# Retention followed by a token-choosing feed-forward: one hand-written order over all 24 chunks

## The chip, the cores and the metric

The kernel runs on one core of a Trainium2 chip. The metric is the device time of one execution in microseconds (us). The core has a matrix engine (TensorE, PE in the profile, with its weight loads PEld), a vector engine (VectorE, DVE), an engine for activations and copies (ScalarE, ACT), a general engine (GpSimd, POOL) and a queue engine for transfers (SyncE, SP). Each engine works through its own queue of instructions in order and waits at the head of it for the semaphores of others. Both SyncE and GpSimd issue DMAs here.

## The reference, cut to what matters

```python
def _attn_ref(q, k, v):                      # each (4, 8, 768, 64): batch, head, token, width
    gamma = 1.0 - 2.0 ** (-5.0 - np.arange(H))
    for t in range(S):
        state = gamma * state + k[:, :, t] (outer) v[:, :, t]
        y[:, :, t] = 1/sqrt(D) * q[:, :, t] @ state

def _moe_ref(x, w_gate, w1, w2, capacity):   # x: (4, 768, 512), the heads side by side
    scores = x @ w_gate                      # one score per token
    out = x.copy()
    for b in range(B):
        top_idx = the 128 tokens of the highest scores
        ye = np.maximum(x[b, top_idx] @ w1, 0.0) @ w2        # 512 -> 1024 -> 512
        g = 1 / (1 + exp(-scores[b, top_idx]))
        out[b, top_idx] = x[b, top_idx] + g[:, None] * ye
```

So each batch is a linear recurrence over 768 tokens with a decaying 64x64 state per head, and then a choice of 128 of the 768 tokens by a score, for which a small feed-forward is added. The whole batch's scores must be known before the choice.

## The kernel before, in words

The 768 tokens of a batch are cut into 6 chunks of 128 tokens. With 4 batches there are 24 chunks. The decay is put into scaled values: `gneg` scales v on its way in, `gpos` scales y on its way out.

*Loads.* k and q of a batch are loaded and cast to bf16 by GpSimd's queue, into tiles with 128 partitions of 6 consecutive tokens each; batch 0 in two halves of 4 heads, the others whole. v is loaded by SyncE's queue in f32, for batch 0 in six pieces by chunk (packets of 256 bytes), for the others whole. `wgb`, the score weights `w_gate` repeated on 128 partitions, comes by SyncE's queue between the third and the fourth piece of v, and w1 and w2 by GpSimd's queue.

*Transposes.* `transpose_qk` (lines 163-173) turns two heads of k or q of a batch into `KT` or `QT` with 12 TensorE transposes and one ScalarE copy; 8 such units make a batch ready.

*A chunk* (`attention`, lines 179-248):
- GpSimd scales v to `Vg` (L183).
- TensorE makes the scores k·q of 8 heads into PSUM tile `pa` (L191), in two halves of 4 matmuls; DVE masks each half to `Am` (L194).
- TensorE forms y in `py` from the earlier state (L201) and from `Am` and `Vg` (L204); DVE scales it to `xo` (L226), SyncE stores it, ScalarE keeps a bf16 copy `xs` (L231).
- TensorE transposes k's rows to `pk` (L210), ScalarE copies them to `Kn`, TensorE adds to the state `U` (L217) and ScalarE copies `U` to `ubd` (L223). The last chunk of a batch leaves this out.
- DVE multiplies `xo` by `wgb` and adds it up to the score column `s6` (the group named `junk`, L235). TensorE spreads the column as a row (`pr`, L238), ScalarE copies it to `srow` (L239), DVE compares all scores so far with this chunk's (`G`, L242), TensorE counts (`pc`, L247), and DVE subtracts the counts from `rank` (L248).

*The feed-forward* (`ffn`, `ffn_store`, lines 250-316) follows a batch's six chunks: DVE builds the choice matrices `P` from `rank`, TensorE gathers the chosen rows (`px`, L267), ScalarE copies them to `xeT`, TensorE gathers places and scores (`pa`, L274), goes up (`ph`, 32 matmuls, L291, with ReLU copies to `hT` on ScalarE) and down (`pe`, 8 matmuls of 512 columns, L304); DVE adds the gated result to `ot` (L310), and GpSimd scatters the rows with an indirect DMA (L312).

*What sets the order.* The program is written batch by batch and chunk by chunk, with the next batch's loads and transposes between the chunks. A list scheduler takes these instructions and sets each engine's order by itself, with the program's order as priority; it allots the slots of the tile pools. The names `psT`, `psA`, `psY`, `psU` and `psF` are pools in PSUM, with 2, 2, 1, 1 and 2 slots of a bank each.

Of the kernel before, what the change touches and what calls it, by code (L numbers as in the profile page):

```python
# [36 lines left out]
def kernel(  # L37
# [27 lines left out]
    ld = ctx.enter_context(tc.tile_pool(name="ld", bufs=B))  # L65
    work = ctx.enter_context(tc.tile_pool(name="work", bufs=3))
    bat = ctx.enter_context(tc.tile_pool(name="bat", bufs=2))
    psT = ctx.enter_context(tc.tile_pool(name="psT", bufs=2, space=bass.MemoryType.PSUM))
    psA = ctx.enter_context(tc.tile_pool(name="psA", bufs=2, space=bass.MemoryType.PSUM))
    psY = ctx.enter_context(tc.tile_pool(name="psY", bufs=1, space=bass.MemoryType.PSUM))  # L70
    psU = ctx.enter_context(tc.tile_pool(name="psU", bufs=1, space=bass.MemoryType.PSUM))
    psF = ctx.enter_context(tc.tile_pool(name="psF", bufs=2, space=bass.MemoryType.PSUM))
# [4 lines left out]
    def load_qk(src, name, tiles, b, h0, h1):  # L77
        if b not in tiles:
            tiles[b] = ld.tile([128, H, J * D], BF, tag=name, name=f"{name}{b}")
        nc.gpsimd.dma_start(tiles[b][:, h0:h1, :],  # L80
                            _view(src[b, h0], [[J * D, 128], [S * D, h1 - h0], [1, J * D]]))

    def load_v(b, c0, c1):
        if b not in vtiles:
            vtiles[b] = ld.tile([128, H, NC, D], FT, tag="v", name=f"v{b}")
        if c1 - c0 == NC:
            ins = nc.sync.dma_start(vtiles[b].rearrange("p h c d -> p (h c) d"),
                                    _view(v[b], [[D, 128], [C * D, H * NC], [1, D]]))
            tc.keep_in_program_order(ins)
        else:  # L90
            for c in range(c0, c1):
                nc.sync.dma_start(vtiles[b][:, :, c, :],
                                  _view(v[b, 0, c * C], [[D, 128], [S * D, H], [1, D]]))

    for h0 in (0, H // 2):
        load_qk(k, "k", ktiles, 0, h0, h0 + H // 2)
        load_qk(q, "q", qtiles, 0, h0, h0 + H // 2)
    load_v(0, 0, 3)

# [51 lines left out]
    load_v(0, 3, NC)  # L151

    w1 = consts.tile([128, ND, F], BF)
    w2 = consts.tile([128, NF, Dm], BF)

# [3 lines left out]


    QTs, KTs = {}, {}

    def transpose_qk(tiles, name, dst, b, dd):
        if b not in dst:
            dst[b] = bat.tile([128, ND, S], BF, tag=name, name=f"{name}{b}")
        tv = tiles[b].rearrange("p h (j d) -> p h j d", j=J)
        pt = psT.tile([128, J, 128], BF, tag="T")
        for j in range(J):
            for sub in range(2):
                nc.tensor.transpose(pt[sub * 64:sub * 64 + 64, j, :], tv[:, 2 * dd + sub, j, :], ident,  # L170
                                    tile_position=(0, sub * 64))
        nc.scalar.activation(dst[b][:, dd, :].rearrange("f (p j) -> f p j", j=J),  # L172
                             pt.rearrange("f j p -> f p j"), AF.Copy)

    for dd in range(ND):
        transpose_qk(ktiles, "KT", KTs, 0, dd)
        transpose_qk(qtiles, "QT", QTs, 0, dd)

    def attention(b, c, st):
        QT, KT = QTs[b], KTs[b]  # L180
        t = slice(c * C, (c + 1) * C)
        Vg = work.tile([128, H, D], BF, tag="Vg")
        nc.gpsimd.tensor_mul(Vg, vtiles[b][:, :, c, :], gneg[:, c, :, None].to_broadcast([128, H, D]))  # L183
        vf = Vg.rearrange("p h d -> p (h d)")

        Ams = []
        for sub in range(2):
            pa = psA.tile([128, ND, 128], FT, tag="A")
            r = slice(sub * 64, sub * 64 + 64)
            for dd in range(ND):  # L190
                nc.tensor.matmul(pa[:, dd, :], KT[r, dd, t], QT[r, dd, t],  # L191
                                 start=True, stop=True)
            Am = work.tile([128, ND, 128], BF, tag=f"Am{sub}")
            nc.vector.tensor_mul(Am, pa, causal4)  # L194
            Ams.append(Am)

        py = psY.tile([128, H, D], FT, tag="y")
        pyf = py.rearrange("p h d -> p (h d)")
        for dd in range(ND):
            if c:  # L200
                nc.tensor.matmul(pyf[:, dd * 128:(dd + 1) * 128], QT[:, dd, c * C:(c + 1) * C],  # L201
                                 Ubd[(c - 1) % 2][:, dd, :], start=True, stop=False)
            for sub in range(2):
                nc.tensor.matmul(py[:, 2 * dd + sub, :], Ams[sub][:, dd, :], Vg[:, 2 * dd + sub, :],  # L204
                                 start=(c == 0), stop=(c == 0 or sub == 1))

        if c < NC - 1:
            pk = psT.tile([128, J, 128], BF, tag="T")
            for dd in range(ND):
                nc.tensor.transpose(pk[:, dd, :], KT[:, dd, t], ident)  # L210
            Kn = work.tile([128, ND, 128], BF, tag="Kn")
            nc.scalar.activation(Kn, pk[:, 0:ND, :], AF.Copy)  # L212
            if c == 0:
                st["U"] = psU.tile([128, ND, 128], FT, tag="U", name="U")
            U = st["U"]
            for dd in range(ND):
                nc.tensor.matmul(U[:, dd, :], Kn[:, dd, :],  # L217
                                 vf[:, dd * 128:(dd + 1) * 128],
                                 start=(c == 0 and dd == 0), stop=(c == NC - 2 and dd == ND - 1),
                                 skip_group_check=True)  # L220
            for sub in range(2):
                r = slice(sub * 64, sub * 64 + 64)
                nc.scalar.activation(Ubd[c % 2][r, :, r], U[r, :, r], AF.Copy)  # L223

# [4 lines left out]
        for sc in scatters:  # L229
            tc.declare_no_dep(base.ins, sc.ins, reason="rows of different batches")  # L230
        nc.scalar.activation(st["xs"][:, c, :], xof, AF.Copy)  # L231

        s6, srow, rank = st["s6"], st["srow"], st["rank"]
        junk = work.tile([128, Dm], FT, tag="junk")
        nc.vector.scalar_tensor_tensor(out=junk, in0=xof, scalar=1.0, in1=wgb, op0=ALU.mult,  # L235
                                       op1=ALU.mult, accum_out=s6[:, c:c + 1])
        pr = psF.tile([128, 512], FT, tag="F")
        nc.tensor.transpose(pr[:, 0:128], s6[:, c:c + 1].to_broadcast([128, 128]), identf)  # L238
        nc.scalar.activation(srow[:, c * C:(c + 1) * C], pr[:, 0:128], AF.Copy)  # L239
        n = (c + 1) * C  # L240
        G = work.tile([128, S], BF, tag="G")
        nc.vector.scalar_tensor_tensor(out=G[:, 0:n], in0=srow[:, 0:n], scalar=s6[:, c:c + 1],  # L242
                                       in1=before[:, S - n:], op0=ALU.is_ge, op1=ALU.mult,
                                       accum_out=st["racc"][:, c:c + 1])
        pc = psF.tile([128, 512], FT, tag="F")
        for j in range(c + 1):
            nc.tensor.matmul(pc[:, j:j + 1], G[:, j * C:(j + 1) * C], ones, start=True, stop=True)  # L247
        nc.vector.tensor_sub(rank[:, 0:c + 1], rank[:, 0:c + 1], pc[:, 0:c + 1])  # L248

    def ffn(b, st):  # L250
        s6, rank, xs = st["s6"], st["rank"], st["xs"]
        nc.vector.tensor_add(rank, rank, st["racc"])
        P = bat.tile([128, NC, 128], BF, tag="P")
        for c in range(NC):
            nc.vector.tensor_scalar(P[:, c, :], sel, rank[:, c:c + 1], None, op0=ALU.is_equal)  # L255
        aux = bat.tile([128, NC, 5], BF, tag="aux")
        rem = bat.tile([128, NC], FT, tag="rem")
        nc.gpsimd.tensor_copy(aux[:, :, 0:2], place_i)
        nc.gpsimd.tensor_copy(aux[:, :, 2], s6)
        nc.gpsimd.tensor_sub(rem, s6, aux[:, :, 2])  # L260
        nc.gpsimd.tensor_copy(aux[:, :, 3], rem)
        nc.gpsimd.tensor_sub(aux[:, :, 4], rem, aux[:, :, 3])

        px = psF.tile([128, 512], FT, tag="F")
        for dd in range(ND):
            for c in range(NC):
                nc.tensor.matmul(px[:, dd * 128:(dd + 1) * 128], xs[:, c, dd * 128:(dd + 1) * 128],  # L267
                                 P[:, c, :], start=(c == 0), stop=(c == NC - 1))
        xeT = bat.tile([128, ND, 128], BF, tag="xeT")
        nc.scalar.activation(xeT, px.rearrange("p (a b) -> p a b", b=128), AF.Copy)  # L270

        pa = psF.tile([128, 512], FT, tag="F")
        for c in range(NC):
            nc.tensor.matmul(pa[:, 0:5], P[:, c, :], aux[:, c, :], start=(c == 0), stop=(c == NC - 1))  # L274
        auxs = bat.tile([128, 5], FT, tag="auxs")
        nc.vector.tensor_copy(auxs, pa[:, 0:5])
        idx = bat.tile([128, 1], I32, tag="idx")
        nc.vector.scalar_tensor_tensor(out=idx, in0=auxs[:, 0:1], scalar=float(b * S),
                                       in1=auxs[:, 1:2], op0=ALU.add, op1=ALU.add)
        ssel = bat.tile([128, 1], FT, tag="ssel")  # L280
        nc.vector.reduce_sum(ssel, auxs[:, 2:5], axis=mybir.AxisListType.X)
        gate = bat.tile([128, 1], FT, tag="gate")
        nc.scalar.activation(gate, ssel, AF.Sigmoid)

        hT = bat.tile([128, NF, 128], BF, tag="hT")
        for half in range(2):
            ph = psF.tile([128, 512], FT, tag="F")
            for f4 in range(4):
                ff = half * 4 + f4
                for dd in range(ND):  # L290
                    nc.tensor.matmul(ph[:, f4 * 128:(f4 + 1) * 128], w1[:, dd, ff * 128:(ff + 1) * 128],  # L291
                                     xeT[:, dd, :], start=(dd == 0), stop=(dd == ND - 1))
# [85 lines left out]
```

## Time and profile before

| what | value |
|---|---|
| time, median of 3 runs | 168.11 us (167.86 to 168.26) |
| the profiled execution | 169.33 us |
| its span, first to last instruction | 167.5 us |
| TensorE busy | 118.1 us (71%), 1412 matmuls |
| VectorE busy | 96.2 us (57%) |
| ScalarE busy | 81.5 us (49%) |
| GpSimd busy | 48.1 us (29%) |
| mean granted TensorE clock | 0.772 of full |
| read from HBM / written | 23.33 MB / 7.34 MB |

The profile comes from one execution. In its page, the second part cuts the span into 40 slices of 4.19 us; a digit is the busy share in tenths, and PEclk the granted TensorE clock in tenths. A group of instructions is written as line, engine, operation, output<-input, shapes and count, then busy time and the mean of one in ns. A timeline row gives the start, the time, the engine and the line, and in brackets the idle time before it with what ended it. TensorE's busy time counts the latency of matmuls that overlap, so it looks fuller than it is.

### The profile page before, as it was taken

How to read it: one execution, taken by the hardware profiler on the slowest of the kernel's cores; microseconds unless marked ns; L12 is line 12 of the kernel's file. 1: busy time of each engine (PE TensorE's matmuls, PEld its weight loads, DVE VectorE, ACT ScalarE, POOL GpSimd, SP SyncE). 2: the span in 40 equal slices, each digit the busy share in tenths (PEclk: the TensorE clock that was granted, in tenths of full speed). 3: DMA queues.
4: the chain of work that ended last, by engine and by line, in shares of the span. 5: the costliest groups of instructions: out<-in, count | busy, mean ns of one | idle time of the engine just before them, and what ended most of it. 6: DMA issues, size and time to landing. Idle time of an engine off the chain costs nothing.

```text
span 167.5 us, 3545 instructions
## 1 busy us (share of the span) xinstructions
PE 118.1 (71%) x1412; PEld 88.1 (53%) x1412; DVE 96.2 (57%) x254; ACT 81.5 (49%) x164; POOL 48.1 (29%) x76
## 2 busy tenths in 40 slices
PE   0028570999999559988867995998479977454870
PEld 0016450676666339766644974766349645234840
DVE  3400031655648896159879708599697299876010
ACT  3015461457554304599981146697821668520230
POOL 7972000626222400072251105222530063010002
PEclk9999996555555555999995579599956999955598
DMA  5999999999999999613111892111301013220001
GB/s 124 175 213 195 191 191 204 207 247 250 251 254 253 230 265 250 148 65 126 70 71 55 217 216 72 63 65 67 125 0 67 0 67 125 86 87 15 4 0 63
DMA packets 24751, 22.50 MB, mean 134 GB/s; under 512 B 6944, under 2 KB 20768, under 8 KB 24736
## 3 DMA queue, kind: packets, MB, share of 16 engines
q0 software_dynamic: 10240, 9.44, 32.9%
q1 hardware_dynamic: 14496, 12.85, 28.8%
q8 instruction: 11, 0.18, 0.4%
q14 instruction: 4, 0.03, 0.1%
HBM read 23.33 MB, written 7.34 MB: 183 GB/s over the span
## 4 chain that ended last, share of the span: by engine, by line
PE 38%; DVE 16%; DMA 14%; ACT 13%; issue 12%; POOL 3%; POOLq 1%; DVEq 0%; ACTq 0%
DMA q<-in_q_dram 13%; PE pt L170 6%; DVE G L242 6%; PE px L267 5%; PE pa L191 5%; PE ph L291 5%; ACT ubd L223 4%; DVE Am L194 4%; DVE junk L235 3%; PE pe L304 3%; PE U L217 3%; PE pr L238 3%; PE py L201 2%; PE py L204 2%; ACT srow L239 2%
## 5 line engine op out<-in xcount | busy, mean ns | idle before, releaser
L194 DVE TENSOR_TENSOR Am<-pa,causal 128x512 bf16<-128x512 f32 x48 | 32.2, 685 | 21.4 <-PE pa L191 19.8
L183 POOL TENSOR_TENSOR Vg<-v,gneg 128x512 bf16<-128x512 f32 x24 | 25.8, 1076 | 53.1 <-PE py L204 21.6
L191 PE MATMUL pa<-QT,KT 64*128 64x128 bf16 x192 | 23.7, 269 | 3.5 <-ACT QT L172 1.8
L242 DVE SCALAR_TENSOR_TENSOR G<-srow,s,before 128x128 bf16<-128x128 f32 (+5 forms) x24 | 20.3, 847 | 9.0 <-ACT srow L239 8.6
L170 PE MATMUL pt<-ident,k 128*64 128x128 bf16 x192 | 13.6, 263 | 11.8 <-DMA k<-in_k_dram 11.1
L226 DVE TENSOR_TENSOR xo<-py,gpos 128x512 f32<-128x512 f32 x24 | 16.5, 686 | 7.8 <-PE py L204 7.6
L231 ACT ACTIVATE xs<-xo 128x512 bf16<-128x512 f32 x24 | 15.1, 628 | 9.9 <-DVE xo L226 9.8
L223 ACT ACTIVATE ubd<-U 64x256 bf16<-64x256 f32 x40 | 15.1, 377 | 9.5 <-PE U L217 8.5
L170 PE MATMUL pt<-ident,q 128*64 128x128 bf16 x192 | 13.6, 270 | 8.3 <-DMA q<-in_q_dram 8.1
L204 PE MATMUL py<-Vg,Am 128*128 128x64 bf16 x192 | 18.3, 218 | 1.2 <-DVE Am L194 0.9
L172 ACT ACTIVATE QT<-pt 128x768 bf16<-128x768 bf16 x16 | 13.0, 813 | 9.8 <-PE pt L170 9.7
L235 DVE SCALAR_TENSOR_TENSOR junk<-xo,wgb 128x512 f32<-128x512 f32 x24 | 17.4, 724 | 0.0
L191 PEld LDWEIGHTS <-KT 64*128 64x128 bf16 x192 | 12.3, 111 | 9.3 <-issue 4.5
L204 PEld LDWEIGHTS <-Am 128*128 128x128 bf16 x192 | 14.9, 115 | 4.2 <-DVE Am L194 2.1
L170 PEld LDWEIGHTS <-k 128*64 128x64 bf16 x192 | 8.8, 131 | 14.8 <-DMA k<-in_k_dram 11.5
L172 ACT ACTIVATE KT<-pt 128x768 bf16<-128x768 bf16 x16 | 12.9, 809 | 6.2 <-PE pt L170 6.0
L201 PE MATMUL py<-ubd,QT 128*128 128x128 bf16 x80 | 14.6, 247 | 1.4 <-DVE xo L226 0.9
L170 PEld LDWEIGHTS <-q 128*64 128x64 bf16 x192 | 9.2, 137 | 10.6 <-DMA q<-in_q_dram 8.7
L312 POOL DMA_INDIRECT out_dram<-ot,idx x4 | 4.4, 1098 | 35.6 <-DVE ot L310 35.6
L212 ACT ACTIVATE Kn<-pk 128x512 bf16<-128x512 bf16 x20 | 11.9, 600 | 4.6 <-PE pk L210 4.5
L267 PE MATMUL px<-P,xs 128*128 128x128 bf16 x96 | 12.5, 303 | 1.3 <-DVE P L255 1.3
L310 DVE SCALAR_TENSOR_TENSOR ot<-pe,gate,xe 128x512 f32<-128x512 f32 x4 | 3.0, 751 | 16.6 <-PE pe L304 16.6
(67 smaller groups left out, 172.1 us busy)
## 6 DMA issues: line engine op xcount, KB each, us to landing
out_dram<-xo SPq DMA_DIRECT2D x24, 256.0 KB, 2.0
k<-in_k_dram POOLq DMA_DIRECT2D x3, 768.0 KB, 18.4
q<-in_q_dram POOLq DMA_DIRECT2D x3, 768.0 KB, 22.4
w<-in_moe_w_dram POOLq DMA_DIRECT2D x2, 1024.0 KB, 29.9
v<-in_v_dram SPq DMA_DIRECT2D x6, 256.0 KB, 13.9
k<-in_k_dram POOLq DMA_DIRECT2D x2, 384.0 KB, 10.5
q<-in_q_dram POOLq DMA_DIRECT2D x2, 384.0 KB, 12.4
wgb<-in_moe_w_gate_dram SPq DMA_DIRECT2D x1, 256.0 KB, 11.9
```

Of the source, the lines that this page charges most:

```text
L170: nc.tensor.transpose(pt[sub * 64:sub * 64 + 64, j, :], tv[:, 2 * dd + sub, j, :], ident, tile_position=(0, sub * 64))
L172: nc.scalar.activation(dst[b][:, dd, :].rearrange("f (p j) -> f p j", j=J), pt.rearrange("f j p -> f p j"), AF.Copy)
L183: nc.gpsimd.tensor_mul(Vg, vtiles[b][:, :, c, :], gneg[:, c, :, None].to_broadcast([128, H, D]))
L191: nc.tensor.matmul(pa[:, dd, :], KT[r, dd, t], QT[r, dd, t], start=True, stop=True)
L194: nc.vector.tensor_mul(Am, pa, causal4)
L201: nc.tensor.matmul(pyf[:, dd * 128:(dd + 1) * 128], QT[:, dd, c * C:(c + 1) * C], Ubd[(c - 1) % 2][:, dd, :], start=True, stop=False)
L204: nc.tensor.matmul(py[:, 2 * dd + sub, :], Ams[sub][:, dd, :], Vg[:, 2 * dd + sub, :], start=(c == 0), stop=(c == 0 or sub == 1))
L223: nc.scalar.activation(Ubd[c % 2][r, :, r], U[r, :, r], AF.Copy)
L226: nc.vector.tensor_mul(xo, py, gpos[:, c, :, None].to_broadcast([128, H, D]))
L235: nc.vector.scalar_tensor_tensor(out=junk, in0=xof, scalar=1.0, in1=wgb, op0=ALU.mult, op1=ALU.mult, accum_out=s6[:, c:c + 1])
L242: nc.vector.scalar_tensor_tensor(out=G[:, 0:n], in0=srow[:, 0:n], scalar=s6[:, c:c + 1], in1=before[:, S - n:], op0=ALU.is_ge, op1=ALU.mul ...
L267: nc.tensor.matmul(px[:, dd * 128:(dd + 1) * 128], xs[:, c, dd * 128:(dd + 1) * 128], P[:, c, :], start=(c == 0), stop=(c == NC - 1))
```

## The change

The list scheduler is switched off by `manual_schedule`: each engine now takes its instructions in the order in which the program writes them. The program is rewritten as one pipeline over n = 0 to 25 (24 chunks and two more rounds), in which each round works on several chunks. The functions of a chunk are cut apart: `scale_v` works two chunks ahead, `scores_kq` and `k_rows` one ahead, `values`, `state` and `score` on chunk n, `score_rows` and `compare` one behind and `count` two behind.

The two half masks become one DVE instruction of 128x1024 over a two-bank tile (`psA` has one slot). The row transpose and the counts share one tile in a new pool `psR` with one slot, and `psF` goes from 2 slots to 1. The feed-forward becomes nine pieces, of which up to three are put at the end of a round from round 14 on; the last batch's nine all follow in round 25.

Batch 0's k and q are loaded in two halves of 64 partitions, which is tokens 0-383 and 384-767, instead of two halves of heads. Its transposes then come in 16 units of half the width. v's pieces 3-5 are issued right behind pieces 0-2, and so ahead of `wgb`. Batches 1 and 2 are asked for at the start, batch 3 in round 5, w1 and w2 in round 3, and the `ld` pool goes from 4 buffers to 3.

```diff
+    ctx.enter_context(tc.manual_schedule())
...
-    for h0 in (0, H // 2):
-        load_qk(k, "k", ktiles, 0, h0, h0 + H // 2)
-        load_qk(q, "q", qtiles, 0, h0, h0 + H // 2)
     load_v(0, 0, 3)
+    for p0 in (0, 64):
+        load_qk(k, "k", ktiles, 0, p0, p0 + 64)
+        load_qk(q, "q", qtiles, 0, p0, p0 + 64)
+    load_v(0, 3, NC)
...
     wgb = consts.tile([128, Dm], FT)
     nc.sync.dma_start(wgb, _view(moe_w_gate, [[0, 128], [1, Dm]]))
...
-    load_v(0, 3, NC)
...
+    load_batch(1)
+    load_batch(2)
...
+        return [choose, gather_a, gather_b, places, rows, lambda: up(0), lambda: up(1), down, store]
...
+    units = {}
+    for b in range(1, B):
+        order = [("KT", dd) for dd in range(ND)] + [("QT", dd) for dd in range(ND)]
+        at = [3, 3, 4, 4, 4, 4, 5, 5] if b == 1 else [0, 0, 1, 1, 2, 2, 3, 4]
+        for c, (which, dd) in zip(at, order):
+            units.setdefault((b - 1) * NC + c, []).append((which, b, dd))
+    late = [("KT", dd) for dd in range(ND)] + [("QT", dd) for dd in range(ND)]
+
+    batch_state(0)
+    scale_v(0)
+    scale_v(1)
+    for dd in range(ND):
+        transpose_qk("KT", 0, dd, 0, 64)
+        transpose_qk("QT", 0, dd, 0, 64)
+    scores_kq(0)
+    k_rows(0)
+
+    pending = []
+    FIRST = 2 * NC + 2
+
+    for n in range(N + 2):
+        b, c = divmod(n, NC)
+        if n < N and c == 0 and b + 1 < B:
+            batch_state(b + 1)
+        if n + 2 < N:
+            scale_v(n + 2)
+        if n == 3:
+            load_weights()
+        if n == 5:
+            load_batch(3)
+        for u in units.get(n, []) if c == NC - 1 else []:
+            transpose_qk(*u)
+        if 1 <= n:
+            pr = psR.tile([128, 512], FT, tag="R")
+        if 2 <= n:
+            count(n - 2, pr)
+        if 1 <= n <= N:
+            score_rows(n - 1, pr)
+        if n + 1 < N:
+            scores_kq(n + 1)
+            k_rows(n + 1)
+        if n < N:
+            xof = values(n)
+            state(n)
+        if 1 <= n <= N:
+            compare(n - 1)
+        if n < N:
+            score(n, xof)
+            if c == 0 and b + 1 < B:
+                load_v(b + 1, 0, NC)
+        if n < 2:
+            for which, dd in late[4 * n:4 * n + 4]:
+                transpose_qk(which, 0, dd, 64, 128)
+        for u in units.get(n, []) if c < NC - 1 else []:
+            transpose_qk(*u)
+        if n >= 2 and (n - 2) % NC == NC - 1:
+            pending += ffn_pieces((n - 2) // NC)
+        if n == N + 1:
+            take = len(pending)
+        elif n >= FIRST:
+            take = min(len(pending), 3)
+        else:
+            take = 0
+        for piece in pending[:take]:
+            piece()
+        pending = pending[take:]
```

The instructions inside `values`, `state`, `score`, `score_rows`, `compare`, `count` and the pieces of the feed-forward are those of the old `attention` and `ffn`, apart from what is said above. The piece `places` now comes after the copy to `xeT`, and `rows` (the transposes of `xeT` back to rows) ahead of the up half.

## The prediction

> **What bounds the kernel now.** I read the page, then VectorE's timeline from end to end, then TensorE's, the chain of waits, GpSimd's and SyncE's timelines, and last the packet records.
>
> ```profile
> span 167.5 us, 3545 instructions
> PE   0028570999999559988867995998479977454870
> DVE  3400031655648896159879708599697299876010
> PEclk9999996555555555999995579599956999955598
> DMA  5999999999999999613111892111301013220001
> ```
>
> Three regimes follow each other. Until 30 us loads rule. From 30 to 67 us TensorE is at half clock and looks full. (The 9s of the first slices stand for no record: 12 transposes take 0.85 at 9.8 as at half clock, 0.53 at 75.4.) After that DVE is the densest engine in the chunk stretches, and each feed-forward (61.9-71, 91.9-102, 125-134, 153-163) leaves it nearly idle. On DVE's timeline the score product (`junk`) of chunk 0 ends at 32.3, of chunk 5 at 60.0, of chunks 11, 17 and 23 at 93.4, 126.7 and 150.1. From there to the span's end are 17.4 us. I write T(n) for that end in chunk n. Batch 1's chunks take about 18 us of their own (72-90), 3 us a chunk, feed-forward apart.
>
> The chain of waits shows the path that the new order puts into every chunk:
>
> ```profile
> 86.99 0.79 DVE junk L235 x2
> 87.78 0.04 issue
> 87.83 0.49 PE pr L238
> 88.34 0.29 ACT srow L239
> 88.65 1.03 DVE G L242 x2
> ```
>
> TensorE's row transpose starts 0.05 after `junk`; here nothing but this batch's end hangs on it. SyncE's two loads, from its timeline, the page's issues and the view of line 92:
>
> ```profile
> 3.73 12.20 SPq L92 DMA_DIRECT2D v<-in_v_dram  x3
> wgb<-in_moe_w_gate_dram SPq DMA_DIRECT2D x1, 256.0 KB, 11.9
> DMA to landing us min/median/max: 3.2/13.9/22.3
> ```
>
> `wgb` goes out at 2.75, ahead of v's chunks 3 to 5, and is there at 14.7. The last piece of v, issued at 10.44 because the queue is full, lands 22.3 later, at 32.7.
>
> **The change, part by part.** The rows say what each engine does in its new order; the sum goes by T(n).
>
> *Start.* In the new order SyncE issues v's chunks 0-2, then 3-5, then `wgb`. `wgb` moves behind 3 DMAs of 1024 packets of 256 B. In the packet records of before SyncE's queue and GpSimd's advance packet for packet, 150-190 each per us from 10 to 26 us; 5840 of v's 6144 packets are through at 26. After, GpSimd's queue stays full (batches 1 and 2 are issued at once, still in 768 B packets), so v ends near 28 and `wgb`'s 128 packets near 29. Engines' rings drift: `wgb`'s last packets came 4 us after the mean of v's packets ahead of it. Bounds 28 and 33 (v's own end before); I take 30.3. `junk`(0) needs it, so T(0) = 31.0.
> Without it: q's first half at 12.5 (the half of the heads landed then, same bytes), 8 half-width evictions from 12.5 at 0.55 (between `srow`'s 0.28 for 128 columns and 0.81 for 768), the last at 17.2; `pa`(0) 1.07, mask 1.13, `pa`(1) (which waits for the one `psA` slot), 4 transposes and values, `xo` 0.6, `junk` 0.7: T(0) = 23.1. So the token halves, the extra evictions and the doubled transposes sit under 8 us of wait and cost nothing (even if loads into 64 partitions crept, and q's half came at 18.5 like the whole q before, T(0) would be 29); if `wgb` is early the 8 us come back. The later weights (first used in chunk 15) and `ld` with 3 buffers (batch 0's tiles are free by chunk 1, asked for in chunk 5) cost nothing, covered by tens of us.
>
> *A plain chunk.* TensorE's order is count(n-2), `score_rows`(n-1), `scores_kq`(n+1), `k_rows`(n+1), values(n), state(n). `score_rows` waits for `junk`(n-1), DVE's last instruction of the round; behind it queue the scores, and DVE's next mask waits for these. So the round is one loop. Half clock, from `junk`(n-1): wait 0.05, transpose 0.37 (its row to the next: 0.34 to 0.41), 8 scores at 0.107 (4 took 0.61 visible), `k_rows` 4 x 0.107, values 0.94 (53.62 to 54.56), 0.25 of latency: `xo` may start at 2.9. The mask (one 128x1024 in place of two 512 of 0.60 start to start) runs 1.5-2.63, so `xo` sets it; `xo` ends at 3.5. Then G, 0.35 to 1.01 with its accumulator read, mean 0.68, and `junk` 0.68: 4.86.
> Full clock: 0.05 + 0.21 + 8 scores 0.6 + mask 1.13 + `xo` 0.6 + G 0.68 + `junk` 0.68 = 4.0.
>
> On top comes GpSimd. `Vg`(n+3) takes the slot that state(n) frees, so it starts at 3.3 in a half-clock round, just ahead of G. Before shows what G does then:
>
> ```profile
> 77.02 1.04 POOL L183 TENSOR_TENSOR Vg<-v,gneg 128x512 bf16<-128x512 f32 x1 [2.18 <-PE U L217]
> 77.27 1.07 DVE L242 SCALAR_TENSOR_TENSOR G<-srow,s,before 128x256 bf16<-128x256 f32 x1
> ```
>
> G of 256 takes 0.48 alone: it lost 0.59 of the 0.79 that `Vg` still had to run. Masks and `xo` beside `Vg` keep 0.68. By this, 0.7 for chunks 1-3, 0.54 for 0 and 4, 0.27 for 5: a batch of half-clock rounds is 32.1, 5.35 each (4.8 to 5.7 if the push is 0 or whole). At full clock `Vg` is over before G: 4.0, batch 24.1. The next batch's transposes come last in TensorE's round: state 0.43 and two units of 12 x 0.055 end it at 4.6 of 5.35, hidden. ACT's own sum, 3.1 to 3.6 a chunk, stays under both.
>
> *The clock.* Rows change at steps of 3.41 us. I counted streamed columns in each step: 64 for a transpose of k or q, half of 128 for a 64-row score matmul.
>
> ```profile
> 33.19:36.60 3.41, 3.41 (x42) 0.50 1.18 244
> 84.40:87.81 3.41, 1.93 (x33) 1.00 0.02 5
> 156.13:159.54 3.41, 2.73 (x29) 0.51 0.00 0
> ```
>
> (PE busy, instructions, clock.) The first, some 2750 columns and a row transpose, is followed by half clock although TensorE looks full; the last, 3077, by full clock; the second, 2100, loses it. The limit lies near 3000 per step. A new round with two batch transposes has 3584: per step 2290 at 5.35, about 3050 at 4.0; without them 2560. Half clock thus sustains itself, full clock only on the edge. A step that falls wholly on the dense part of a round passes, about a third of them: I take 1/3 of the rounds to chunk 13 at full clock, bounds none and all from chunk 3.
> The Trainium skill ("TensorE: Matmul & The Clock Gate", Why this matters for your kernels) says that the full clock is lost to idle gaps of over about 3 us. By that the new rounds, with gaps near 1 us, would stay full; this trace speaks against it: 84.4-87.8 has no gap over 0.8 and loses it.
>
> T(13): 13 rounds, 69.4 at half clock, +1 for the late transposes in chunk 1 and the four in chunk 4, less a third of the 17.2 between the clocks: 64.7, so T(13) = 95.7. Before stood at 60.0 after chunk 5, the new order stands near 57; at 93.4 after chunk 11, now near 86, with two feed-forwards still owed.
>
> *Feed-forward*, three pieces a round in chunks 14-22. It no longer stands alone, but its pieces sit in TensorE's queue ahead of the next `score_rows`. Full clock, extra over a plain round: choose 1.3 (6 x 0.21) and then 18 gather matmuls at 0.057 that DVE waits for, 1.1; `auxs` after `junk`, then 16 up matmuls, 1.1; second up half, wait for its ReLU (one `psF` slot), 8 down matmuls of 0.216 and `ot`, 1.6. Three rounds 12.06 + 5.1 = 17.2; at half clock 25 (16.05 + 3.4 + 1.9 + 3.65). With 3930 columns more a round most steps pass: 80% full, 18.8. Three batches 56.3: T(22) = 152.0 (147.3 to 170.7 at the two clocks); one more round 5.0: T(23) = 157.0.
>
> *Tail.* Before 17.4 from T(23). With one `psF` slot the places wait for `xeT` and the first up half for `auxs`, +1.0; each ReLU now stands between two groups, +0.85 and +0.7; the gaps can keep the clock at half for the down group (+1.7), half counted: 20.4. The span is 177.4. The profiled execution took 169.3 with a span of 167.5, the median is 168.1: 177.4 + 1.8 - 1.2 = **178.0**.
>
> **Rivals.**
> *Full clock* from chunk 3 on (what the skill's rule would give): T(2) = 42.3, 11 rounds 44.7, T(13) = 86.9; then 51.6, 4.2, tail 19.3: span 162.0, time 162.6, faster. It decides if steps hold some 3000 columns; for it 135.6-142.4, where 3500 a step held; against it 30-57.
> *`wgb` not late*: 8 us off: 170. For it, only if small DMAs pass v; against, its own drift before.
> *Half clock throughout, feed-forward too*: T(13) 101.4, 66 for three batches at 22, 5.3, tail 21.5: 194, time 195.
> *The order is not kept as written*, and the scores go ahead of the row transpose: no loop; DVE's own work bounds it, 96.2 busy less 5.3 before 30 us: 31 + 91 + 17 = 139. The diff itself speaks against it.
>
> **How the numbers follow.** Forecast 0.58 (own range 168 to 187: push 4.8-5.7, `wgb` 28-33, mix of clocks), full clock 0.17, `wgb` early 0.10 (a third of it faster), half clock throughout 0.10, other order 0.05. Low end 161 takes in the full clock, high end 189 half of the slow case's way. Faster by over 0.2% (about what a measurement of this kernel tells from none): 0.17 + 0.05 + 0.03 = 0.25, less 0.02 for slow full-clock cases: 0.23. Within: 0.03. Slower: 0.74.
>
> **What would show it.** Right: `junk` of chunk 0 ends near 31 released by the DMA of `wgb`; DVE's mask waits 1.0 to 1.5 for `pa` in every chunk; G of 1 us beside `Vg`; PEclk at 5 until about 95 with a few exceptions, then mostly 9; the last `junk` near 157 and 20 us after it. Wrong: rounds of under 4.5 before chunk 13, a first `junk` before 25, or rounds of 8 with feed-forward.

## The result: 11.8% slower

The new order takes 187.64 us (median of 4 runs, 186.85 to 193.25) against 167.99 for the kernel before on the same chip; the ratio is 1.118, with an interval of 1.1061 to 1.130. A kernel's executions now and then run at a lower clock and some per cent longer; the ratios leave those out, medians do not, and the profiles below of `wgb` early, of ten slots for `Vg` and of before with `wgb` late are of such executions. The profiled execution took 186.88, with a span of 184.8. The forecast was 178.0 with a range of 161 to 189.

The page of the kernel after:

```profile
span 184.8 us, 3685 instructions
PE   0047702768665767664787966457687397744760
DVE  0602301767827786787778565766364833656010
PEclk9999999999975699876555999965559755795798
DMA  6999999998999999311395011110110201120001
```

The nines of PEclk before 46 us stand for no record, as they do in the page of before: eight score matmuls take 0.62 at 43.1, as at half clock, and 0.41 at 48.1.

VectorE (DVE) is never empty between 30 and 165 us and never full: mostly 5 to 8 tenths of a slice. The deep holes of before, one for each feed-forward, are gone, and with them the dense chunk stretches. TensorE (PE) looks alike. Each engine waits a little in every round. By T(n), the end of the score product in chunk n:

| us | T(0) | T(5) | T(13) | T(22) | T(23) | T(23) to the end |
|---|---|---|---|---|---|---|
| forecast | 31.0 | 57 | 95.7 | 152.0 | 157.0 | 20.4 |
| after | 31.31 | 60.31 | 96.22 | 160.32 | 166.48 | 18.3 |

Before had T(23) = 150.08 and a tail of 17.4: 16.4 of the 17.3 us that the span grew lie ahead of the last score product.

*Start.* DVE's timeline, then SyncE's (start, duration, line, what was issued):

```profile
30.61 0.69 DVE L273 SCALAR_TENSOR_TENSOR junk<-xo,wgb 128x512 f32<-128x512 f32 x1 [9.76 <-DMA wgb<-in_moe_w_gate_dram]
```

```profile
0.81 13.42 SPq L95 DMA_DIRECT2D v<-in_v_dram  x6
14.27 5.37 SPq L147 DMA_DIRECT2D wgb<-in_moe_w_gate_dram  x1
```

`xo` of chunk 0 was ready at 20.8, and `junk` waited 9.76 for `wgb`, which went out at 14.27, behind all six pieces of v, and was there 16.2 later.

*A plain round*, number 3, at half clock. DVE's timeline, then GpSimd's:

```profile
43.74 1.22 DVE L218 TENSOR_TENSOR Am<-pa,causal 128x1024 bf16<-128x1024 f32 x1 [1.14 <-PE pa L215]
45.11 0.69 DVE L246 TENSOR_TENSOR xo<-py,gpos 128x512 f32<-128x512 f32 x1 [0.15 <-PE py L243]
45.72 1.38 DVE L288 SCALAR_TENSOR_TENSOR G<-srow,s,before 128x384 bf16<-128x384 f32 x1
...
47.03 0.68 DVE L273 SCALAR_TENSOR_TENSOR junk<-xo,wgb 128x512 f32<-128x512 f32 x1
...
47.64 0.15 DVE L298 TENSOR_TENSOR rank<-rank,pr 128x3 f32<-128x3 f32 x1
```

```profile
45.65 1.04 POOL L205 TENSOR_TENSOR Vg<-v,gneg 128x512 bf16<-128x512 f32 x1 [2.37 <-PE U L261]
```

The mask waits 1.14 for the scores, which stand behind the row transpose; then DVE has only a gap of 0.15 to the round's end. G takes 1.38 because `Vg` started 0.07 ahead of it. The chain of waits, summed over the run (total, times, longest):

```profile
DVE Am L218 <- PE pa L215: 30.6, 24, 8.1
...
DVE rank L298 <- PE pr L297: 15.7, 9, 3.5
...
PE pr L279 <- DVE rank L298: 9.9, 23, 0.9
```

The mask waits in all 24 chunks: 8.1 in the first, 22.5 in the other 23, 0.98 each. The third line the forecast did not have: the row transpose writes into the same PSUM tile `pr` as the counts, so it also waits until DVE has subtracted the counts from `rank`, one DVE instruction behind `junk`.

*Feed-forward.* A piece stands at the end of its round and so delays the chunk behind it: the pieces of rounds 14 to 22 fall between T(14) and T(23), three rounds a batch. The windows of the three batches (columns: length; busy time of PE, PE's weight loads, DVE, ACT, GpSimd; granted clock; share of DMA; GB/s):

```profile
101.20:120.81 19.61, 12.26 (x186) 9.14 (x186) 12.24 (x35) 11.54 (x22) 4.65 (x7) 1.00 0.14 52
120.81:144.80 23.99, 16.66 (x169) 13.21 (x169) 13.13 (x34) 9.38 (x20) 5.52 (x10) 0.64 0.11 39
144.80:166.47 21.67, 15.28 (x155) 12.25 (x154) 11.87 (x33) 7.43 (x16) 2.51 (x5) 0.67 0.15 55
```

The first batch takes 19.6 at full clock, the other two 24.0 and 21.7 at a lower one. On DVE's timeline, what opens the second batch's feed-forward:

```profile
120.93 2.08 DVE L312 TENSOR_SCALAR P<-sel,rank 128x128 bf16<-128x128 f32 x6
125.40 0.16 DVE L298 TENSOR_TENSOR rank<-rank,pr 128x5 f32<-128x5 f32 x1 [2.39 <-PE pr L297]
```

The six choice matrices take 2.08 (1.27 in the first batch, at 101.33); GpSimd works on `Vg` beside them, from 121.10 to 122.14. Then DVE waits 2.39 for the count, which TensorE does only after the gather matmuls.

### The profile page after: what moved, and what is told of

Same layout as the page of the kernel before. It is cut to its first block, busy times and chain, and to the rows that moved or that the text cites. A ratio compares the mean times of both kernels' runs of the same rounds, so it can differ in the third digit from the quotient of the medians.

```text
span 184.8 us, 3685 instructions
## 1 busy us (share of the span) xinstructions
PE 111.2 (60%) x1508; PEld 86.6 (47%) x1508; DVE 97.8 (53%) x230; ACT 86.5 (47%) x172; POOL 47.3 (26%) x76
## 3 DMA queue, kind: packets, MB, share of 16 engines
q0 software_dynamic: 10240, 9.44, 30.5%
## 4 chain that ended last, share of the span: by engine, by line
PE 31%; DVE 27%; issue 18%; DMA 9%; SPq 7%; ACT 5%; POOLq 1%; POOL 0%; DVEq 0%; ACTq 0%
DVE G L288 9%; DMA wgb<-in_moe_w_gate_dram 9%; DVE xo L246 7%; SPq L95 7%; DVE junk L273 6%; PE pa L215 6%; PE pr L279 5%; PE px L328 4%; PE ph L366 4%; PE pe L374 3%; PE pk L227 2%; PE py L243 2%; PE py L240 2%; DVE P L312 2%; DVE rank L298 1%
## 5 line engine op out<-in xcount | busy, mean ns | idle before, releaser
L218 DVE TENSOR_TENSOR Am<-pa,causal 128x1024 bf16<-128x1024 f32 x24 | 29.4, 1225 | 30.6 <-PE pa L215 30.6
L288 DVE SCALAR_TENSOR_TENSOR G<-srow,s,before 128x128 bf16<-128x128 f32 (+5 forms) x24 | 23.4, 976 | 0.9 <-ACT srow L280 0.9
L273 DVE SCALAR_TENSOR_TENSOR junk<-xo,wgb 128x512 f32<-128x512 f32 x24 | 16.4, 683 | 9.8 <-DMA wgb<-in_moe_w_gate_dram 9.8
L279 PE MATMUL pr<-identf,s 128*128 128x128 f32 x24 | 9.9, 411 | 17.9 <-DVE rank L298 9.9
L266 ACT ACTIVATE ubd<-U 64x256 bf16<-64x256 f32 x40 | 15.1, 378 | 11.4 <-PE U L261 10.4
L280 ACT ACTIVATE srow<-pr 128x128 f32<-128x128 f32 x24 | 6.7, 279 | 26.2 <-PE pr L279 26.0
L246 DVE TENSOR_TENSOR xo<-py,gpos 128x512 f32<-128x512 f32 x24 | 16.4, 685 | 2.1 <-PE py L243 1.2
L181 PE MATMUL pt<-ident,k 128*64 128x128 bf16 (+1 forms) x240 | 11.2, 260 | 10.5 <-DMA k<-in_k_dram 9.3
L243 PEld LDWEIGHTS <-Am 128*128 128x128 bf16 x192 | 16.2, 124 | 0.0
L181 PEld LDWEIGHTS <-k 128*64 128x64 bf16 (+1 forms) x240 | 9.6, 147 | 11.8 <-DMA k<-in_k_dram 9.3
L181 PE MATMUL pt<-ident,q 128*64 128x128 bf16 (+1 forms) x240 | 11.2, 251 | 6.3 <-DMA q<-in_q_dram 2.2
L184 ACT ACTIVATE QT<-pt 128x768 bf16<-128x768 bf16 (+1 forms) x20 | 13.0, 681 | 3.6 <-PE pt L181 3.4
L184 ACT ACTIVATE KT<-pt 128x768 bf16<-128x768 bf16 (+1 forms) x20 | 12.8, 680 | 3.9 <-PE pt L181 3.7
L366 PE MATMUL ph<-xeT,w 128*128 128x128 bf16 x128 | 11.3, 259 | 5.1 <-DVE auxs L343 4.4
L328 PEld LDWEIGHTS <-xs 128*128 128x128 bf16 x96 | 9.2, 127 | 11.1 <-issue 9.4
## 6 DMA issues: line engine op xcount, KB each, us to landing
wgb<-in_moe_w_gate_dram SPq DMA_DIRECT2D x1, 256.0 KB, 16.2
```

Source lines behind the costliest of these rows:

```text
L181: nc.tensor.transpose(pt[sub * 64:sub * 64 + 64, j, 0:n], tv[p0:p1, 2 * dd + sub, j, :], ident[p0:p1, p0:p1], tile_position=(p0, sub * 64))
L184: nc.scalar.activation(dst[b][:, dd, p0 * J:p1 * J].rearrange("f (p j) -> f p j", j=J), pt[:, :, 0:n].rearrange("f j p -> f p j"), AF.Copy)
L218: nc.vector.tensor_mul(Am.rearrange("p a b t -> p (a b) t"), pa.rearrange("p a b t -> p (a b) t"), causal[:, None, :].to_broadcast([128, H ...
L243: nc.tensor.matmul(py[:, 2 * dd + sub, :], Am[:, sub, dd, :], Vg[:, 2 * dd + sub, :], start=(c == 0), stop=(c == 0 or sub == 1))
L246: nc.vector.tensor_mul(xo, py, gpos[:, c, :, None].to_broadcast([128, H, D]))
L279: nc.tensor.transpose(pr[:, 0:128], st["s6"][:, c:c + 1].to_broadcast([128, 128]), identf)
```

## The experiments

The theory: (1) `wgb` in SyncE's queue costs the start 9 us; (2) written as it is, TensorE's order makes each round one loop through the row transpose, and `Vg` pushes G on it; (3) the granted clock follows the columns that TensorE streams per step of 3.41 us, and the new rounds stream too few; (4) feed-forward pieces stall the queues in which they stand. The diffs are shortened: conditions are left out, and three dots stand for arguments.

**`wgb` early.** The load is moved between v's chunk 2 and chunk 3.

```diff
     load_v(0, 0, 3)
+    wgb = consts.tile([128, Dm], FT)
+    nc.sync.dma_start(wgb, ...)          # was behind load_v(0, 3, NC)
```

> Only wgb is issued between v's pieces 2 and 3, as it was before. Theory (wgb late gates the first round, and the rest just shifts): the first junk starts near 22 to 23 us in place of 30.6 and the whole span shrinks by about 7.5 us, time near 179.5. Rival (the rounds after are held by other loads, k and q of batch 1 or v of batch 1): the wait turns up again within the first six rounds and less than 3 us is left, 184 or more.

Ratio to before 1.089 [1.0796, 1.0983], against 1.118: 4 to 5 us come back, not 8 or 9. T(0) = 22.20, 9.1 earlier, but T(5) = 56.84, only 3.5 earlier. SyncE's timeline and the chain of waits of this kernel show where the rest went:

```profile
20.96 0.36 SPq L248 DMA_DIRECT2D out_dram<-xo  x1
21.54 0.83 SPq L91 DMA_DIRECT2D v<-in_v_dram  x1
26.51 33.72 SPq L248 DMA_DIRECT2D out_dram<-xo  x6
```

```profile
POOL Vg L205 <- DMA v<-in_v_dram: 7.6, 1, 7.6
...
DVE xo L246 <- DMA out_dram<-xo: 4.7, 1, 4.7
```

The next batch's whole v goes out right behind the first store, and the later stores stand behind it; with three slots, `xo` of chunk 4 waited 4.7 for a store to finish. That was read off the trace, so it was put to the test.

**`wgb` early and six slots for `xo`.**

```diff
+    xop = ctx.enter_context(tc.tile_pool(name="xop", bufs=6))
-        xo = work.tile([128, H, D], FT, tag="xo")
+        xo = xop.tile([128, H, D], FT, tag="xo")
```

> wgb between v's pieces 2 and 3, and six buffers for xo in place of three. With wgb early alone the first round ended 9.1 us earlier but 5.6 were lost again in rounds 3 to 5, where xo waited 4.7 for the store of an earlier xo that stood behind v of batch 1 in SyncE's queue. Theory (that store is what took the gain): xo waits for no store, and the time is 177 to 180. Rival (v of batch 1, at 42.9 us, holds the pipeline anyway, through Vg): only 1 to 2 us more are won, 182 or more.

178.60 us (177.74 to 179.54), ratio 1.0526 [1.0428, 1.0623]. T(0) = 20.94, T(5) = 51.58, T(23) = 156.11: the 8.7 us are still there in chunk 5 and 10.4 at the end. The kernel after has no wait of `xo` for a store, so the six slots alone would not have helped it. So (1) is shown, and so is the store behind v that took part of it back.

**Before, with `wgb` late.** Only that load is moved, in the kernel before.

```diff
     load_v(0, 0, 3)
-    wgb = consts.tile([128, Dm], FT)
-    nc.sync.dma_start(wgb, ...)
     load_v(0, 3, NC)
+    wgb = consts.tile([128, Dm], FT)
+    nc.sync.dma_start(wgb, ...)
```

> The kernel before with only wgb moved behind v's chunks 3 to 5 in SyncE's queue. Theory (before, the first score product waits for whole q and its eviction and ends at 32.3, so wgb landing at 29 to 33 is hidden or nearly; the late wgb costs 9 us only where the half loads would have let the first chunk start at 22): the first product ends at 32-33.5, the time stays within 1 us of before, 167-169. Rival (a late wgb costs some us in any order): 171 or more.

```profile
32.20 0.69 DVE L235 SCALAR_TENSOR_TENSOR junk<-xo,wgb 128x512 f32<-128x512 f32 x1 [1.35 <-DMA wgb<-in_moe_w_gate_dram]
```

DVE's timeline: the first score product waits 1.35 and ends at 32.90 instead of 32.27. The median is 169.75 (165.79 to 171.52) against 169.15 beside it, with no interval, but nothing near 9 us. The same place in the queue is nearly free where whole q is awaited anyway, and costs 9 us where half of q would have let chunk 0 start.

**Scores and values ahead of count and row transpose.**

```diff
-            count(n - 2, pr); score_rows(n - 1, pr)
-            scores_kq(n + 1); k_rows(n + 1); xof = values(n)
+            scores_kq(n + 1); k_rows(n + 1); xof = values(n)
+            count(n - 2, pr); score_rows(n - 1, pr)
             state(n)
```

> Only the order within a round changes: scores and k_rows of the next chunk and the values come first on TensorE, then count and score_rows, then the state. Theory (the loop junk, row transpose, scores, mask is the cost): the mask's wait for pa (0.78 or 1.14 in every round, 30.6 in all, 8 of it the first) falls below 0.3, plain rounds take 3.6 to 4.2 in place of 5.0, and the time falls by 15 to 22 us, to 165 to 172. Rival (TensorE at half clock or ScalarE is as slow as the loop): the wait only moves to xo or G, rounds stay above 4.6, and the gain is under 9 us, 178 or more.

200.16 us (199.41 to 201.12), ratio 1.1873 [1.181, 1.1937]: the expectation fell. The chain of waits of this kernel:

```profile
DVE Am L218 <- PE pa L215: 32.4, 13, 7.8
...
PE pr L279 <- DVE rank L298: 24.7, 23, 2.1
...
DVE G L288 <- ACT srow L280: 18.7, 23, 0.9
```

and a group by line of it:

```profile
L273 DVE SCALAR_TENSOR_TENSOR junk<-xo,wgb 128x512 f32<-128x512 f32 x24 | 23.2, 965 | 9.9 <-DMA wgb<-in_moe_w_gate_dram 9.9
```

The mask waits in 13 chunks instead of 24, as meant, though not for less in all. But the row transpose now waits 24.7 for the rank subtraction, which DVE does behind `xo`, and G waits 0.8 for `srow` in every round. The loop went through the shared tile `pr` and came back longer, 70.7 from T(0) to T(13) against 64.9. A second cost comes with it: since G now starts later, `Vg` meets `junk` instead, which takes 1.52 in place of 0.68 in eight rounds up to T(13). In all `junk` grows from 16.4 to 23.2 while G falls only from 23.4 to 20.8. How much of the 12.8 us over the kernel after each of the two costs, no run separates. Joined with the early `wgb`, where the two gains were to add:

> Both edits, wgb early and the new order within a round. If the two costs are separate, the gains add up: 7.5 and 15 to 22, time 158 to 165, faster than the kernel before. Rival: with shorter rounds the loads of batch 1 (k landed near 24, q near 30 us, v near 41) become the wait, and less than half of the 7.5 is left, 165 to 170.

199.46 us, ratio 1.175 [1.1686, 1.1813]: T(0) = 21.83, but T(5) = 61.81; a round of 13.35 in chunk 4, in which `xo` waited 7.4 for a store, took it all.

**Scores first, then the count, and the row transpose behind the values.**

```diff
+            scores_kq(n + 1)
             count(n - 2, pr)
-            score_rows(n - 1, pr); scores_kq(n + 1); k_rows(n + 1); xof = values(n)
+            k_rows(n + 1); xof = values(n); score_rows(n - 1, pr)
             state(n)
```

> Order within a round: scores of the next chunk, count, k_rows, values, then score_rows, then state. In the run that put count and score_rows together behind the values, the row transpose waited for DVE's subtraction from rank (both use one PSUM tile), which DVE did only after xo. Here count comes early, so the subtraction follows the mask. Theory (the loop is what costs a round, and that run only made a new one): the transpose waits for rank under 0.3, plain rounds are 4.0 to 4.7, time 172 to 180. Rival (TensorE's strict order costs whatever stands first, because something always waits behind a late operand): rounds near 5 again, 185 or more.

Median 181.92 us (178.3 to 183.16) where 172 to 180 was expected; no interval. The chain of waits:

```profile
DVE Am L218 <- PE pa L215: 30.6, 12, 8.0
...
PE pr L279 <- DVE rank L298: 9.3, 13, 1.6
```

T(0) to T(13) takes 58.3 instead of 64.9, rounds of 2.9 to 4.6 without the batch transposes: 0.5 a round is what the row transpose ahead of the scores costs, net of the push, which partly moves to `junk` here too (20.6 against 16.4). The transpose still waits 0.7 for the rank subtraction in 13 rounds, where under 0.3 was expected. The feed-forward rounds are untouched: T(14) to T(23) 65.2 here, 65.3 after. So the row transpose's part of (2) is supported, with a smaller price than the whole loop.

**`Vg` away from G.** Ten slots for `Vg`, in a pool of its own, instead of three.

> The kernel after with ten buffers for Vg instead of three, so that GpSimd's scaling starts as soon as v is there and not when a state update frees a slot, which is just before G. Theory (the push of G by Vg lies on the loop of each round, 7.1 us in all by G's own rows): G's busy time falls from 23.4 to 17-19 us and the time by 4 to 6 us, to 181-184. Rival (the rounds' end is set elsewhere, by the mask's wait and the transpose's wait for the rank subtraction, or Vg meets other DVE work instead): G gets shorter, the time moves by less than 2 us.

The groups by line of this kernel, where G stood at 23.4 and a mean of 976 ns after:

```profile
L289 DVE SCALAR_TENSOR_TENSOR G<-srow,s,before 128x128 bf16<-128x128 f32 (+5 forms) x24 | 17.1, 713 | 0.7 <-ACT srow L281 0.7
```

Ratio 1.0805 [1.0709, 1.0902], below the 1.118 of after with intervals apart: G is 6.3 us shorter, and the time follows by some 4 to 6. The push lay on the path, as forecast. Part of it moved: P grew from 6.7 to 8.3 and `junk` from 16.4 to 18.1, so DVE's work shrank by 3.0 in all, less than the time did; where the rest comes from is not shown.

**Fill the clock's steps.** Ten matmuls of 256 columns, with a result nobody reads, at the end of rounds 1 to 13.

```diff
+        if 1 <= n <= 13:
+            for _ in range(10):
+                nc.tensor.matmul(pr[:, 256:512], ident, before[:, 0:256], start=True, stop=True)
```

> The changed kernel with 10 more matmuls of 128x256 at the end of each of rounds 1 to 13; they write columns of the row transpose's tile that nobody reads, and change no result. TensorE gets 2560 columns a round to stream more, 1.1 us at full clock and 2.1 at half. Theory (the clock of the next 3.41 us goes by the columns streamed, limit near 3000): rounds 1 to 13 run at full clock nearly throughout, about 4.0 each in place of 5.0, time 175 to 180 although TensorE has more to do. Rival (the clock goes by idle gaps, which are short already, or the clock does not set the round): the clock stays mixed and the rounds are as long or up to 1 us longer, 187 to 200.

The page's row of the granted clock:

```profile
PEclk9999999999999999999998799965559755795798
```

With more columns the clock is full from the first record, at 45.4, to T(13) (46.6 to 94.4: 1.00, against 0.74 after in the same rounds); from slice 22 on, where nothing was added, the row is nearly that of after. So added matmuls raise the clock. They also shorten TensorE's gaps; that the columns and not the gaps count is read from the steps of after, below.

The time hardly followed: median 185.81 (183.12 to 189.15), no interval, T(13) = 94.43 instead of 96.22, where 175 to 180 us was expected. From T(2) to T(13) the kernel gained 4.1 us (49.6 against 53.7). But in the first two rounds TensorE was still at half clock: ten of the added matmuls took 2.32 at 37.1 and 1.27 at 47.8, and the way from T(1) to T(2) grew from 6.37 to 8.72. A good part of the gain goes through `Vg`: G fell from 23.4 to 19.6, since at full clock `Vg` is mostly over before G starts.

**Feed-forward spread out**, from round 8 and two pieces a round, instead of 14 and three.

```diff
-    FIRST = 2 * NC + 2
+    FIRST = 8
-            take = min(len(pending), 3)
+            take = min(len(pending), 2)
```

> The kernel after with one change: the feed-forward pieces may start in round 8 instead of 14 and come two a round instead of three. Theory (the 9 us that the forecast missed are clock and crowding: three pieces a round make TensorE wait for the choice matrices and lose the full clock, while rounds 8 to 13 without pieces stream too few columns to gain it): rounds 8 to 13 get enough columns, T(7) to T(23) falls from 97.2 to 80-90 us, the time to 172-181. Rival (each piece costs about 1.1 us of queueing wherever it stands, (65.3 - 9 x 4.0) / 27): T(7) to T(23) stays at 94-99 and the time within 2 us of the kernel after.

183.64 us (182.53 to 183.72), ratio 1.0845 [1.077, 1.0919]. The same 17 rounds, T(6) to T(23), with the same 27 pieces, first of after, then here. Windows of after:

```profile
65.48:166.48 101.00, 69.92 (x896) 54.62 (x896) 65.02 (x152) 53.26 (x106) 23.05 (x34) 0.74 0.29 84
```

and of the spread kernel:

```profile
64.88:162.13 97.25, 63.99 (x893) 49.60 (x896) 66.66 (x152) 52.75 (x106) 22.48 (x32) 0.82 0.29 85
```

The clock rises from 0.74 to 0.82 and 3.75 us come back, where the theory had 7 to 17 and its rival some 3 at most. So most of a piece's cost travels with it. The gain fits the clock, but the pieces also stand apart now, and this run does not separate the two. A round with `choose` still takes 8.1 (T(14)).

**The list scheduler on the changed program.** The one line that asks for the written order is taken out.

```diff
-    ctx.enter_context(tc.manual_schedule())
```

> The changed program without manual_schedule: loads, pieces, pools and program order as after the change, but a list scheduler sets each engine's order again. Theory (the strict order is what costs): the scores move ahead of the row transpose, the mask's wait shrinks, time 165 to 175. Rival (the one-slot pools and the load order cost, whatever the order): 180 or more.

164.33 us (163.11 to 166.99), ratio 0.9741 [0.9653, 0.9829]: faster than before by its interval, though not surely by 2%. So the rest of the change taken together is no loss, and the written order alone costs some 23 us (means of 187.4 and 163.9 over the runs in the ratios). The mask's waits fall from 30.6 to 10.5 in all. This version has a stall of its own. SyncE's and DVE's timelines:

```profile
19.83 17.85 SPq L90 DMA_DIRECT2D v<-in_v_dram  x2
37.77 16.20 SPq L247 DMA_DIRECT2D out_dram<-xo  x2
```

```profile
58.92 0.69 DVE L245 TENSOR_TENSOR xo<-py,gpos 128x512 f32<-128x512 f32 x1 [19.54 <-DMA out_dram<-xo]
```

Two loads of v went out ahead of the stores, and `xo` of chunk 3 found no free slot for 19.5 us.

**List scheduler, `wgb` early, six slots for `xo`**: the three edits above together.

> The changed program with the list scheduler, wgb early and six buffers for xo. With the list scheduler alone it took 163 to 164, of which xo waited 19.5 us for a store that stood behind two loads of v in SyncE's queue. Theory (that wait is on the path): 148 to 156, faster than the kernel before. Rival (the stall hides loads that would be waited for next, k, q and v of batch 1 and the weights): 158 to 163.

154.91 us (154.0 to 157.41), ratio 0.9094 [0.8982, 0.9207]: 9% faster than before, and the fastest that was run. Its chain of waits still has

```profile
DVE xo L246 <- DMA out_dram<-xo: 15.9, 2, 10.4
```

**The same, with v of the next batch in six pieces**, one in each chunk, meant to let stores through between them.

```diff
-            if c == 0 and b + 1 < B:
-                load_v(b + 1, 0, NC)
+            if b + 1 < B:
+                load_v(b + 1, c, c + 1)
```

> The list scheduler's order on the changed program, with wgb early and six xo buffers (154.9 us), and now v of the next batch loaded in six pieces, one in each chunk, instead of whole in chunk 0. Theory (the 15.9 us that xo waits there for stores are stores standing behind 6144 packets of v in SyncE's queue): the wait of xo falls under 4 us, the time to 142-150. Rival (behind that wait other waits come next, for the batch's transposes or the feed-forward, or v in pieces comes too late for Vg): 152 or more.

159.97 us (159.39 to 160.91), ratio 0.9482 [0.9419, 0.9545]: slower than the version it came from, and the expectation fell. SyncE's timeline:

```profile
3.63 64.36 SPq L95 DMA_DIRECT2D v<-in_v_dram  x15
68.10 1.44 SPq L248 DMA_DIRECT2D out_dram<-xo  x2
```

The scheduler gave SyncE 15 pieces of v in a row and the first store at 68.1; `xo` waited 26.5 at one go. That fits stores behind v as the stall, from the wrong side; the edit did not reach what it was aimed at. It also changed the packets: in the packet records a whole v goes out as 1536 packets of 1 KB, in six pieces as 6144 of 256 bytes (the expectation counts 6144 for the whole load too). Stores on a queue of their own were not tried.

## Why the prediction was right

The loop, the late `wgb` and the push of G are there as forecast, and the time lies inside the stated range, near its upper end. It lies just past the 168 to 187 that the forecast gave to its own case, because the feed-forward term was 9 us too small.

- *Start* (31.0; 31.31): right in size and cause. `wgb` landed near 30.5, forecast 30.3; early, T(0) is 20.9 to 22.2, forecast 23.1.
- *Plain rounds* (T(13) 95.7; 96.22): the loop was as described. Apart from two rounds that stand behind four units of transposes, the rounds take 3.76 to 4.09 at full clock (forecast 4.0) and 4.85 to 5.2 at half (5.35). The exact sum owes something to luck: five rounds of 13 ran at full or mostly full clock where 4.3 were assumed, and those two were under-priced: T(1) to T(2) took 6.37 and T(4) to T(5) took 8.65, some 5 us over plain ones, where the sum had 1 us. In the second TensorE waits for ScalarE's copies of 0.75, with two PSUM slots for four units, and DVE then waits 3.48 for the count.
- *Push of G by `Vg`*: forecast 0.27 to 0.7 a round at half clock, none at full. After, G over 384 columns takes 1.38 in the half-clock round shown above, and 0.62 in the kernel with scores first; at full clock it takes 0.55 to 0.81 in chunks 6 to 8, still 0.2 over the 0.34 to 0.61 of chunks 18 to 20, which no `Vg` meets. G lost 6.3 us of 23.4 when `Vg` was moved.
- *The clock*: the rule held. The columns are counted from the trace's matmuls by the step of 3.41 us in which they start, with 64 for a transpose of k or q and for a score matmul. In after, each step that streamed 3072 columns or more was followed by full clock, each with 2722 or fewer by half; between 2816 and 2950 both occur. One step of the feed-forward, as a window:

```profile
132.05:135.46 3.41, 3.15 (x40) 2.65 (x38) 1.41 (x3) 1.47 (x3) 0.00 (x0) 0.50 0.00 0
```

 TensorE is busy for 3.15 of 3.41, with some 2820 to 2950 columns by where the step is cut, and the step after it is still at half clock. The step from 111.4 is the other way round: busy for 1.74 of 3.41, with a gap of 1.68 and 3840 columns, and full clock follows. So neither busy time nor gaps sort the steps, and columns do. The Trainium skill ("TensorE: Matmul & The Clock Gate", Why this matters for your kernels) names idle gaps of over about 3 us as what takes the full clock away; here it was also lost behind a step with no gap over 0.8 (from 80.7, 2180 columns).

 The forecast's count for a round with two units of transposes, 3584 columns, is too low by its own rule: 2560 and 24 transposes of 64 make 4096. Such a round holds full clock with room to spare (T(6) to T(7): 4225 columns in 3.76 us, 3835 a step) and at half clock stays under the limit on the average (T(11) to T(12): 3718 in 5.17, 2455 a step), so that only a step on its dense part regains it. That about a third of the rounds had full clock does not follow from 3584; it was a guess that came out well.
- *Feed-forward rounds*: the term that was mis-sized. The forecast put the three batches in T(13) to T(22), at 56.3, and a plain round of 5.0 behind them. The plain round comes first, T(13) to T(14), 4.99, and the batches take 65.3, T(14) to T(23): the term was 9.0 too small, where the whole span missed by 7.4. Most of it is the share of full clock, set at 80%: by the clocks of the three windows, between 0.5 and 1, it was 100%, 28% and 34%, and the forecast's own prices, 17.2 and 25, then make 17.2, 22.8 and 22.3, 6 us more than 56.3. The other 3 are the prices: the first batch took 19.6 at full clock, not 17.2. The forecast counted on 3930 more columns a round and did not see that the gather stands at the head of TensorE's queue until DVE is through with `xo`, G, `junk` and the first choice matrix: TensorE is idle for 2.98 up to 121.28, and the step from 118.3 to 121.7 streams 128 columns. The half-clock steps behind it stream 2945, 2722, 1536 and 2950. The spread kernel fits the clock as a part of this; it does not show how large a part.
- *The tail* (20.4; 18.3) misses by -2.1 and hides some of that. The forecast's terms for it add up to 20.8, not 20.4.
- *What would show it*: of the signs for right, the first three came as written, but the mask's wait is 0.78 at full clock, less than 1.0. The PEclk sign came out wrong in its order: full clock was common from 46 to 82 us, and of the two longest half-clock stretches one, 84.1 to 101.2, lies mostly in the plain rounds and the other, 121.7 to 138.7, in the feed-forward. The last `junk` came at 166.5, not near 157. Two of the three signs for wrong came as well: five rounds of under 4.5 before chunk 13, and rounds of 9.8 and 9.0 with feed-forward. The first came with the mix of clocks, which the sum allowed for; the second belongs to the mis-sized term.

Of the rivals, full clock from chunk 3 and an order not kept are excluded by the PEclk row and the mask's 24 waits, and `wgb` not late by its landing. Half clock throughout came nearest in the feed-forward, with 66 for the three batches; its 22 a batch is not the 25 that the forecast's sum has for half clock.

## What to carry to other kernels

An order written by hand turns every place in a queue into a dependency: before writing one, list for each engine what stands ahead of the instruction that the next engine waits for, DMA queues and shared PSUM tiles included, and sum the loop that this closes. Here a scheduler's order on the same program was 23 us better, and moving one load and adding three buffers was worth 9 more. Moving one instruction out of such a loop helps only if the loop does not close again through another tile; change one place, then read the chain of waits.

## What was not expected of the hardware

- A store behind a load of v on one queue holds its buffer until the load is through: the longest wait was 4.7 and 7.4 us behind one load, 19.5 and 10.4 behind two (the second with six slots), and 26.5 behind 15 pieces.
- P, with a single tile and a column of scalars as input, is also pushed by GpSimd: 2.08 instead of 1.27 for six. So is `junk`, with 1.52 instead of 0.68 where `Vg` runs beside it.
- TensorE's clock could be bought with useless columns: 4.1 us gained where they ran at full clock, 2.4 lost where they ran at half.
